# Attention followed by a mixture of experts: temporaries of the token choice in PSUM, the logit add between two scans, and a new written order at a step's and the attention's end

## The chip, the cores and the metric

The kernel runs on one core of one Trainium2 chip. The metric is the device time of one execution in microseconds. A core has five engines with an instruction stream each, which work side by side and wait for one another through semaphores: TensorE (PE, with its weight loads shown apart as PEld), VectorE (DVE), ScalarE (ACT), GpSimd (POOL) and SyncE (SP, here only DMA issues).

## The reference

Two layers follow each other. The first is a gated linear attention with a decay for each channel; the second sends each of 3072 tokens to one of 8 experts, at most 384 to each, in the order of falling logits.

```python
# q, k, v, alpha: (4 batches, 8 heads, 768 positions, 48 channels), float32
for t in range(S):
    state = alpha[:, :, t, :, None] * state + einsum('bhd,bhe->bhde', k[:, :, t], v[:, :, t])
    y[:, :, t] = einsum('bhd,bhde->bhe', q[:, :, t], state)
x = y as (3072, 384)
logits = x @ w_gate                     # (3072, 8)
for idx in argsort(-logits.flatten()):  # greedy: best pair of token and expert first
    tok, e = idx // 8, idx % 8
    if the token has an expert or the expert has 384 tokens: continue
    assigned[tok] = e
for e in range(8):                      # w1: 384 x 1024, w2: 1024 x 384
    out[assigned == e] = relu(x[assigned == e] @ w1[e]) @ w2[e]
```

## The kernel before

**Attention.** The positions are cut into chunks of 128, the heads taken in pairs. A *step* `s` is one pair of heads over four chunks; there are NS = 24 of them, in NG = 6 groups of HP = 4 steps (a group is one set of 512 tokens, its four steps the four pairs). The loop runs over `i`, and in its body stands work of several steps, so that engines overlap:

- PE: the key transposes of step i (`keys`, L237), logits of step i-2 (`logits`, L313), scores of step i (L245), outputs of step i-1 (L294 from the carried state, L300 from the masked scores), and the states of step i (L267).
- DVE: `carry(i-1)` (L283, L285: the running state, chunk by chunk), `add_logits(i-2)` (L319, L321), `decay(i+2)` (two scans over the decays, L211 and L214, with a reciprocal L213 between them), and a piece of the token choice.
- ACT: the scaled states `sb` (L278), the evacuations `kn` (L238), `sm` (L253) and `yt` (L308).
- POOL: the causal mask of step i-1 (L257), the scaled keys and queries of step i+1 (L218, L224), and some clearing of tables (L130).
- SP: the loads of step i+4.

**The token choice.** When a group's four steps have their logits, PE turns them (`turn_logits`, L324), and DVE does the first round of the search ahead of time for these 512 tokens (`first_choice`): the best logit of each token and a one-hot of its expert, the logit's bits as a sortable key, the key cut into five digits, and a table `cmp` that compares the first digit with 128 thresholds. It is a generator with three pieces, one for each loop step: L348 to L351, then L353 to L143 (`digits` is a helper), then L358 and L360. In the step after that, `first_counts` lets PE count with `cmp` as weights (L372) and DVE add the counts up (L377). The last group's choice comes behind the loop.

**PSUM.** One tile `bank` (named `st` in the rows) holds the states' products, the logits, the turned logits and the counts. Another tile, `aux`, has 1024 words a row; 904 of them are filled at the start (zeros and ones, which the scans read, and the reciprocals).

**What sets the order.** Inside `tc.manual_schedule` PE, DVE, ACT and POOL run in the order in which the code is written. Behind the loop, the end of the attention is outside that block: a scheduler orders it. There, `fill(n)` emits `y_trans`, which turns the outputs of a step to token-major form (L332 on PE, L335 on ACT) and every fourth time writes a group to DRAM (L338 on ACT's queue). The numbers `Y_BEFORE_...` say how many of them stand before which part; the rest are spread over the first search (L541 to L623), where four tables are searched one after another. Then eight experts follow, each with gathered rows, weights split into two parts, and two layers of matmuls (L799, L819).

Of the kernel before, what the change touches and what calls it, by code (L numbers as in the profile page):

```python
# [18 lines left out]
WARM_IN_ROUTE = (6, 4, 2, 2)  # L19
Y_BEFORE_CHOICE = 1  # L20
Y_BEFORE_LOGITS = 2
Y_BEFORE_COUNTS = 5
# [6 lines left out]
def gla_moe_kernel(ctx, tc, q, k, v, alpha, w_gate, w1, w2, out):  # L29
# [107 lines left out]

    def digits(key, out_, pool, n):
        di = pool.tile([128, nb, n], I32, name=f"di{n}")
        nc.vector.tensor_tensor(di, key[:, None, :].to_broadcast([128, nb, n]), shifts[:, :, :n],  # L140
                                op=OP.logical_shift_right)
        nc.vector.tensor_tensor(di, di, masks[:, :, :n], op=OP.bitwise_and)
        nc.vector.scalar_tensor_tensor(out_, di, 1.0, scale[:, :, :n], op0=OP.add, op1=OP.mult)  # L143
# [33 lines left out]
    nc.vector.memset(wg, 0.0)  # L177

# [24 lines left out]
    def decay(s):  # L203
# [3 lines left out]
        scans(a, sc, ga, 0, 4)  # L207

    def scans(a, sc, ga, u, n):
# [130 lines left out]
    def first_choice(g):  # L340
        sl = slice(4 * g, 4 * g + 4)
        lw = L[:, sl]
        m = work.tile([128, 4], F32, name="m0")
        val = work.tile([128, 4, E], BF, name="val0")
        sg = work.tile([128, 4], I32, name="sg0")
        key = work.tile([128, 4], I32, name="key0")
        cmp = CM[g] = work.tile([128, T, 4], BF, name="cmp0")
        nc.vector.tensor_copy(lw, lgp[:, :, :E])  # L348
        nc.vector.tensor_reduce(m, lw, axis=mybir.AxisListType.X, op=OP.max)
        nc.vector.tensor_tensor(val, lw, m[:, :, None].to_broadcast([128, 4, E]), op=OP.is_equal)  # L350
        nc.vector.tensor_scalar(sg, m.bitcast(I32), 31, -2 ** 31, op0=OP.arith_shift_right, op1=OP.bitwise_or)  # L351
        yield
        nc.vector.tensor_mul(val, val, ramp_b[:, sl])  # L353
        nc.vector.tensor_tensor(key, m.bitcast(I32), sg, op=OP.bitwise_xor)
# [3 lines left out]
        nc.vector.tensor_tensor(o0[:, sl], ramp_b[:, sl], chu0[:, sl, None].to_broadcast([128, 4, E]),  # L358
                                op=OP.is_equal)
        nc.vector.tensor_tensor(cmp, dig0[:, None, 0, sl].to_broadcast([128, T, 4]), iota, op=OP.is_ge)  # L360
        yield

    def first_counts(g):
        if g == NG - 1:
            fill(Y_BEFORE_COUNTS)
# [4 lines left out]
        with tc.issue_after(YM[NS - len(late) - 1].ins) if last else ExitStack():  # L370
            for u in range(4):
                nc.tensor.matmul(fcp[:, 0 if last else u], CM[g][:, :, u], o0[:, 4 * g + u],  # L372
                                 start=u == 0 or not last, stop=u == 3 or not last)
# [49 lines left out]
    with tc.manual_schedule(engines={E_.DVE, E_.PE, E_.Activation, E_.Pool}):  # L423
# [3 lines left out]
        for i in range(NS + 1):  # L427
# [8 lines left out]
            if i < NS:  # L436
# [6 lines left out]
                keep_scores(i)  # L443
            if i >= 2:
# [21 lines left out]
    fill(Y_BEFORE_LOGITS)  # L466
    logits(NS - 1)
    fill(1)
    add_logits(NS - 1)
    fill(Y_BEFORE_CHOICE)  # L470
    turn_logits(NG - 1)
    for _ in first_choice(NG - 1):
        pass
    first_counts(NG - 1)
# [436 lines left out]
```

## Time and profile before

| | |
|---|---|
| time, median of 3 runs | 462.52 us (461.09 to 462.57) |
| the profiled execution | 460.07 us, its span 458.4 us |
| busy share of the span | PE 89%, PEld 77%, DVE 66%, ACT 43%, POOL 60% |
| granted TensorE clock, mean | 0.948 |
| chain that ended last, by engine | PE 62%, DVE 21%, DMA 6%, issue 6%, ACT 2% |
| attention loop from step 5 to its end | 33.21 to 141.34 us |

"Busy" is the time in which an engine has an instruction in work, a wait for a resource included once it has begun. The chain is followed back from the last instruction, at each step to what released it. In the timeline a row has the start in us from the span's start, the duration in us, engine, line and operation, what is written and read, the count of merged instructions, and in brackets how long the engine was idle before and what ended it. In rows of groups the numbers behind the bar are the busy time in us, the mean of one in ns, and the idle time before.

### The profile page before, as it was taken

To read this page: it belongs to the slowest core of one execution; us is meant where nothing else is said; L and a number is where in the kernel's file an instruction comes from. 1 tells how busy PE (TensorE), PEld (TensorE's weight loads), DVE (VectorE), ACT (ScalarE), POOL (GpSimd) and SP (SyncE) were. 2 spreads that over 40 slices of the span, in tenths; PEclk is the share of its full clock that TensorE was granted. 3 is DMA by queue.
4 is the path that set the end of the run, shared out by engine and by line. 5 is a ranking of instruction groups with operands and counts; after the bars stand their busy time and mean duration, and the time that the engine had idled before them with its cause. 6 is when DMAs were issued, how large, how long until landed. Compare 5 with 4: busy or idle time off the path is not lost.

```text
span 458.4 us, 10845 instructions
## 1 busy us (share of the span) xinstructions
PE 407.5 (89%) x4142; PEld 353.2 (77%) x4142; DVE 304.1 (66%) x837; ACT 196.1 (43%) x447; POOL 275.7 (60%) x300
## 2 busy tenths in 40 slices
PE   7998696968799847997799999999999999899993
PEld 3786575756577734997788889989889889799993
DVE  8789899898963585576558767767768767421210
ACT  2385455545466523416224424524524524444511
POOL 4578776656651006466474964784784786798702
PEclk8599999999999975999899899999999999999998
DMA  8999654653000674136108208108208108920101
GB/s 297 310 264 257 177 164 145 172 165 107 1 4 34 244 259 152 57 101 227 53 1 305 75 1 295 67 19 291 74 19 303 60 19 301 332 73 0 53 2 52
DMA packets 34468, 63.40 MB, mean 138 GB/s; under 512 B 3328, under 2 KB 14592, under 8 KB 34416
## 3 DMA queue, kind: packets, MB, share of 16 engines
q1 hardware_dynamic: 28176, 48.54, 33.4%
q0 software_dynamic: 3072, 9.44, 6.4%
q10 hardware_dynamic: 3168, 4.72, 2.9%
q8 instruction: 33, 0.54, 0.5%
q14 instruction: 19, 0.16, 0.1%
HBM read 53.25 MB, written 9.44 MB: 137 GB/s over the span
## 4 chain that ended last, share of the span: by engine, by line
PE 62%; DVE 21%; DMA 6%; issue 6%; ACT 2%; POOL 1%; POOLq 0%; SPq 0%; DVEq 0%; ACTq 0%
PE h L799 20%; PE y L819 19%; PE rt L590 6%; DVE ga L214 4%; DVE sc L211 4%; DMA raw_a<-in_alpha_dram 4%; PE y L300 3%; DMA xr<-x_dram,idx 3%; PE y L294 3%; PE xt L332 2%; DVE cmp L541 2%; PE xt L783 2%; PE s L245 1%; PE xt L724 1%; PE xt L237 1%
## 5 line engine op out<-in xcount | busy, mean ns | idle before, releaser
L759 POOL TENSOR_TENSOR wlo<-w2r,whi 128x384 fp32r<-128x384 f32 x64 | 64.9, 1015 | 29.9 <-DVE cmp L541 28.4
L803 ACT ACTIVATE hh<-h 128x384 fp32r<-128x384 f32 x64 | 31.4, 491 | 103.0 <-PE h L799 94.1
L759 POOL TENSOR_TENSOR wlo<-w1r,whi 128x384 fp32r<-128x384 f32 x64 | 64.8, 1012 | 8.0 <-ACT whi L753 5.7
L731 POOL DMA_INDIRECT xr<-x_dram,idx x24 | 32.2, 1341 | 62.0 <-DVE scr L648 30.1
L819 PE MATMUL y<-wlo,hh 128*128 128x384 f32 x192 | 66.4, 346 | 0.0
L819 PE MATMUL y<-whi,hh 128*128 128x384 f32 x192 | 66.4, 346 | 0.0
L819 PE MATMUL y<-whi,hl 128*128 128x384 f32 x192 | 65.0, 339 | 0.0
L804 DVE SCALAR_TENSOR_TENSOR hl<-h,hh 128x384 fp32r<-128x384 f32 x64 | 35.5, 554 | 38.8 <-ACT hh L803 34.3
L257 POOL TENSOR_SCALAR_AFFINE_SELECT sm<-sm 128x512 f32<-128x512 f32 x48 | 29.4, 637 | 49.1 <-ACT sm L253 49.1
L753 ACT ACTIVATE whi<-w1r 128x384 fp32r<-128x384 f32 x64 | 32.2, 522 | 53.3 <-PE y L819 37.6
L799 PE MATMUL h<-xh,wlo 128*128 128x384 f32 x192 | 48.8, 354 | 0.0
L799 PE MATMUL h<-xh,whi 128*128 128x384 f32 x192 | 47.0, 352 | 1.9 <-DVE hl L804 0.7
L799 PE MATMUL h<-xl,whi 128*128 128x384 f32 x192 | 48.6, 354 | 0.0
L278 ACT ACTIVATE sb<-st,sc 128x48 f32<-128x48 f32 x80 | 24.5, 331 | 48.1 <-DVE st L285 28.8
L830 POOL DMA_INDIRECT out_dram<-yt,idx x24 | 27.8, 1158 | 26.1 <-ACT yt L823 21.5
L799 PEld LDWEIGHTS h<-xh,whi 128*128 128x128 f32 x192 | 34.3, 194 | 5.6 <-issue 1.8
L541 DVE TENSOR_TENSOR cmp<-nd,iota 128x1536 bf16<-128x1536 bf16 (+4 forms) x32 | 37.4, 1179 | 0.7
L590 PEld LDWEIGHTS <-cmp 128*128 128x128 bf16 x816 | 30.4, 118 | 8.4 <-DVE cmp L541 5.7
L819 PEld LDWEIGHTS y<-wlo,hh 128*128 128x128 f32 x192 | 36.2, 188 | 0.1
L819 PEld LDWEIGHTS y<-whi,hh 128*128 128x128 f32 x192 | 36.1, 188 | 0.1
L819 PEld LDWEIGHTS y<-whi,hl 128*128 128x128 f32 x192 | 36.1, 188 | 0.0
L799 PEld LDWEIGHTS h<-xh,wlo 128*128 128x128 f32 x192 | 35.8, 197 | 0.0
(169 smaller groups left out, 830.8 us busy)
## 6 DMA issues: line engine op xcount, KB each, us to landing
w1r<-in_moe_w_dram SPq DMA_DIRECT2D x16, 768.0 KB, 4.8
w2r<-in_moe_w_dram SPq DMA_DIRECT2D x16, 768.0 KB, 6.4
vt<-in_v_dram SPq DMA_DIRECT2D x24, 256.0 KB, 3.8
x_dram<-xg ACTq DMA_DIRECT2D x6, 768.0 KB, 3.8
raw_a<-in_alpha_dram SPq DMA_DIRECT2D x19, 226.2 KB
raw_k<-in_k_dram SPq DMA_DIRECT2D x19, 224.0 KB
raw_q<-in_q_dram SPq DMA_DIRECT2D x19, 224.0 KB, 3.8
raw_a<-in_alpha_dram SPq DMA_DIRECT2D x5, 258.5 KB, 4.8
```

The lines of the kernel that those rows point to most:

```text
L257: nc.gpsimd.affine_select(SM[s][:, h], SM[s][:, h], pattern=[[0, 4], [1, C]], compare_op=OP.is_ge, fill=0.0, base=0, channel_multiplier=-1)
L278: nc.scalar.activation(SB[s, u][:, :D], St[p], AF.Copy, scale=ac)
L541: x = nc.vector.tensor_tensor(words(dst, nt, js), keyed(d, nt, js), each(iotas[t], nt, js), op=OP.is_ge)
L590: nc.tensor.matmul(cnt, cmp[:, j // U, :, j % U], o[:, j], start=(j == 0), stop=(j == NU - 1))
L731: last_gather[0] = nc.gpsimd.indirect_dma_start(out=XR[i][:, b], out_offset=None, in_=x_dram, in_offset=bass.IndirectOffsetOnAxis(ap=IDX[i ...
L753: nc.scalar.activation(hi[:, 0], a, AF.Copy)
L759: y = nc.gpsimd.tensor_sub(lo[:, h], x, hi[:, h])
L799: nc.tensor.matmul(o, a[:, 0, d], x[:, d], start=(n == 0), stop=(n == 3 * DB - 1))
L803: nc.scalar.activation(hh, o, AF.Relu)
L804: nc.vector.scalar_tensor_tensor(hl, o, 0.0, hh, op0=OP.max, op1=OP.subtract)
L819: F2[i, q] = nc.tensor.matmul(Y[b], a[:, bs], w[:, 1].rearrange("p a b -> p (a b)"), start=(q == 0 and n == 0), stop=(q == FB - 1 and n == 2))
L830: st_ = nc.gpsimd.indirect_dma_start(out=out, out_offset=bass.IndirectOffsetOnAxis(ap=IDX[i][:, b:b + 1], axis=0), in_=yt, in_offset=None)
```

## The change

The temporaries of `first_choice` (the maximum, the one-hot, the key, the digits) and a copy of the small ramp of expert numbers move from SBUF to unused words of `aux` in PSUM; the compare is now an add and a compare in one instruction that reads the digit from there. `add_logits` moves between the first scan and the reciprocal. In a loop step, the scaled keys and queries and the outputs are written ahead of the turn, the choice and the counts. What stood behind the loop is now inside the manual block, with other numbers of `fill`, and the count of the last group has no ordering edge any more.

```diff
+Y_BEFORE_OUTPUTS = 2
+Y_BEFORE_LOGITS = 1
 Y_BEFORE_CHOICE = 1
-Y_BEFORE_LOGITS = 2
-Y_BEFORE_COUNTS = 5
+Y_BEFORE_COUNTS = 4
...
+        nc.vector.tensor_copy(ramp_p, ramp)
+        yield
...
-    def digits(key, out_, pool, n):
...
+    spare = [W4 + 3 * 129]
+
+    def own(n, dt=F32):
+        x = aux[:, spare[0]:spare[0] + n]
+        spare[0] += n
+        return x if dt is F32 else x.bitcast(dt)
+
+    ramp_p, best, key0 = own(E), own(4), own(4, I32)
+    val0 = own(4 * E).rearrange("p (u e) -> p u e", e=E)
+    dig_p = own(nb * 4, I32).rearrange("p (t u) -> p t u", u=4)
...
     def scans(a, sc, ga, u, n, last=-1):
...
+        if last >= 0:
+            add_logits(last)
         nc.vector.reciprocal(aux[:, lo:hi:129], sc[:, lo + 1:hi + 1:129])
...
     def first_choice(g):
...
-        nc.vector.tensor_reduce(m, lw, axis=mybir.AxisListType.X, op=OP.max)
-        nc.vector.tensor_tensor(val, lw, m[:, :, None].to_broadcast([128, 4, E]), op=OP.is_equal)
-        nc.vector.tensor_scalar(sg, m.bitcast(I32), 31, -2 ** 31, op0=OP.arith_shift_right, op1=OP.bitwise_or)
+        nc.vector.tensor_reduce(best, lw, axis=mybir.AxisListType.X, op=OP.max)
+        nc.vector.tensor_tensor(val0, lw, best[:, :, None].to_broadcast([128, 4, E]), op=OP.is_equal)
+        sg = work.tile([128, 4], I32, name="sg0")
+        nc.vector.tensor_scalar(sg, best.bitcast(I32), 31, -2 ** 31, op0=OP.arith_shift_right, op1=OP.bitwise_or)
         yield
-        nc.vector.tensor_mul(val, val, ramp_b[:, sl])
-        nc.vector.tensor_tensor(key, m.bitcast(I32), sg, op=OP.bitwise_xor)
-        nc.vector.tensor_reduce(chu0[:, sl], val, axis=mybir.AxisListType.X, op=OP.max)
-        digits(key, dig0[:, :, sl], work, 4)
+        nc.vector.tensor_mul(val0, val0, ramp_b[:, sl])
+        nc.vector.tensor_tensor(key0, best.bitcast(I32), sg, op=OP.bitwise_xor)
+        nc.vector.tensor_reduce(chu0[:, sl], val0, axis=mybir.AxisListType.X, op=OP.max)
+        nc.vector.tensor_tensor(dig_p, key0[:, None, :].to_broadcast([128, nb, 4]), shifts[:, :, :4],
+                                op=OP.logical_shift_right)
         yield
-        nc.vector.tensor_tensor(o0[:, sl], ramp_b[:, sl], chu0[:, sl, None].to_broadcast([128, 4, E]),
-                                op=OP.is_equal)
-        nc.vector.tensor_tensor(cmp, dig0[:, None, 0, sl].to_broadcast([128, T, 4]), iota, op=OP.is_ge)
+        nc.vector.tensor_tensor(dig_p, dig_p, masks[:, :, :4], op=OP.bitwise_and)
+        nc.vector.scalar_tensor_tensor(dig0[:, :, sl], dig_p, 1.0, scale[:, :, :4], op0=OP.add, op1=OP.mult)
+        nc.vector.tensor_tensor(o0[:, sl], ramp_p[:, None, :].to_broadcast([128, 4, E]),
+                                chu0[:, sl, None].to_broadcast([128, 4, E]), op=OP.is_equal)
+        nc.vector.scalar_tensor_tensor(cmp, dig_p[:, None, 0].to_broadcast([128, T, 4]), 1.0, iota,
+                                       op0=OP.add, op1=OP.is_ge)
         yield
...
-        if g == NG - 1:
-            fill(Y_BEFORE_COUNTS)
...
-        with tc.issue_after(YM[NS - len(late) - 1].ins) if last else ExitStack():
...
             if i >= 2:
-                add_logits(i - 2)
                 if (i - 2) % HP == HP - 1:
                     turn_logits((i - 2) // HP)
-            if i + 2 < NS:
-                decay(i + 2)
-            if i >= 2:
-                if (i - 2) % HP == HP - 1:
                     choosing = first_choice((i - 2) // HP)
                 next(choosing, None)
                 if i > HP + 2 and (i - 2) % HP == 2:
                     first_counts((i - 2) // HP - 1)
-            if 1 <= i < NS - 1:
-                scale_k(i + 1)
-                scale_q(i + 1)
-            if i >= 1:
-                run(outputs(i - 1))
-                emit(i - 1)
```

Ahead of that piece now stand `decay(i + 2, i - 2)` (or `add_logits(i - 2)` where no decay is left), `scale_k` and `scale_q`, at `i == NS` a `fill(Y_BEFORE_OUTPUTS)`, and `outputs(i - 1)` with `emit(i - 1)`; behind it, as before, `states(i)`. The end is, one indent deeper than before:

```python
        fill(Y_BEFORE_LOGITS)
        logits(NS - 1)
        fill(Y_BEFORE_CHOICE)
        add_logits(NS - 1)
        turn_logits(NG - 1)
        for _ in first_choice(NG - 1):
            pass
        fill(Y_BEFORE_COUNTS)
        first_counts(NG - 1)
```

The line numbers of the changed file are 4 to 8 higher. The first place is DVE in step 5, where a group's first choice piece runs, before:

```order
L321 TENSOR_TENSOR lt_180<-lt_180,st 128x128
L211 SCALAR_TENSOR_TENSOR sc<-raw_a_123,aux 128x516
L213 RECIPROCAL aux<-sc 128x4
L214 SCALAR_TENSOR_TENSOR ga<-raw_a_123,aux 128x516
L348 COPY L<-st 128x32
L349 TENSOR_REDUCE m_641<-L 128x4
L350 TENSOR_TENSOR val_642<-L,m_641 128x32
L351 TENSOR_SCALAR sg_643<-m_641 128x4
```

and after (L217, L221, L222 are the scans and the reciprocal, L329 the add, L352 to L356 the piece; `aux` is the PSUM tile):

```order
L217 SCALAR_TENSOR_TENSOR sc<-raw_a_123,aux 128x516
L329 TENSOR_TENSOR lt_180<-lt_180,st 128x128
L221 RECIPROCAL aux<-sc 128x4
L222 SCALAR_TENSOR_TENSOR ga<-raw_a_123,aux 128x516
L352 COPY L<-st 128x32
L353 TENSOR_REDUCE aux<-L 128x4
L354 TENSOR_TENSOR aux<-L,aux 128x32
L356 TENSOR_SCALAR sg_666<-aux 128x4
```

The add has moved behind the first scan, and the piece's results are in `aux`. The second place is PE in the same step, before:

```order
L313 MATMUL st<-yt,wg 32x128 x4
L245 MATMUL s<-qh,kh 128x128 x8
L324 MATMUL st<-ident,lt_180 128x128
L294 MATMUL y<-qh,sb_164 64x128 x2
L294 MATMUL y<-qh,sb_165 64x128 x2
L294 MATMUL y<-qh,sb_167 64x128 x2
L300 MATMUL y<-sm_160,vt 48x128 x4
L300 MATMUL y<-sm_160,vt 64x128 x2
L300 MATMUL y<-sm_160,vt 48x128 x2
L267 MATMUL st<-vt,kn 48x48 x6
```

and after (L302 and L308 are the outputs, L332 the turn, L275 the states):

```order
L253 MATMUL s<-qh,kh 128x128 x8
L302 MATMUL y<-qh,sb_164 64x128 x2
L302 MATMUL y<-qh,sb_165 64x128 x2
L302 MATMUL y<-qh,sb_167 64x128 x2
L308 MATMUL y<-sm_160,vt 48x128 x4
L308 MATMUL y<-sm_160,vt 64x128 x2
L308 MATMUL y<-sm_160,vt 48x128 x2
L332 MATMUL st<-ident,lt_180 128x128
L275 MATMUL st<-vt,kn 48x48 x6
```

The turn has moved from ahead of the outputs to between outputs and states. The third place is PE in step 8, where a group is counted, before:

```order
L267 MATMUL st<-vt,kn 48x48 x6
L237 MATMUL xt<-ident,kh 128x128 x4
L313 MATMUL st<-yt,wg 32x128 x4
L245 MATMUL s<-qh,kh 128x128 x8
L372 LDWEIGHTS cmp_645
L372 MATMUL st<-o_102,cmp_645 128x8
```

and after (L378 is the count):

```order
L253 MATMUL s<-qh,kh 128x128 x8
L302 MATMUL y<-qh,sb_168 64x128 x2
L302 MATMUL y<-qh,sb_169 64x128 x2
L302 MATMUL y<-qh,sb_171 64x128 x2
L308 MATMUL y<-sm_161,vt 48x128 x4
L308 MATMUL y<-sm_161,vt 64x128 x2
L308 MATMUL y<-sm_161,vt 48x128 x2
L378 LDWEIGHTS cmp_662
L378 MATMUL st<-o_102,cmp_662 128x8
```

The counts, which followed the scores, now follow the outputs; each is four weight loads with a matmul.

More of the change, by code (lines that the diff above doesn't have):

```diff
@@ L206, in decay, with scans @@
         ga = GA[s] = work.tile([128, W4], F32, name="ga", bufs=3)
-        scans(a, sc, ga, 0, 4)
-    def scans(a, sc, ga, u, n):
+        scans(a, sc, ga, 0, 4, last)
+    def scans(a, sc, ga, u, n, last=-1):
         lo, hi, top = 129 * u, 129 * (u + n), W4 + 3 * 129
@@ L369, in first_counts @@
             nc.vector.tensor_scalar(need, need, -1.0, float(CAP), op0=OP.mult, op1=OP.add)
-        with tc.issue_after(YM[NS - len(late) - 1].ins) if last else ExitStack():
-            for u in range(4):
-                nc.tensor.matmul(fcp[:, 0 if last else u], CM[g][:, :, u], o0[:, 4 * g + u],
-                                 start=u == 0 or not last, stop=u == 3 or not last)
+        for u in range(4):
+            nc.tensor.matmul(fcp[:, 0 if last else u], CM[g][:, :, u], o0[:, 4 * g + u],
+                             start=u == 0 or not last, stop=u == 3 or not last)
         if last:
@@ L443, in gla_moe_kernel @@
                 keep_scores(i)
+            if i + 2 < NS:
+                decay(i + 2, i - 2)
+            elif i >= 2:
+                add_logits(i - 2)
+            if 1 <= i < NS - 1:
+                scale_k(i + 1)
+                scale_q(i + 1)
+            if i == NS:
+                fill(Y_BEFORE_OUTPUTS)
+            if i >= 1:
+                run(outputs(i - 1))
+                emit(i - 1)
             if i >= 2:
[L445 removed]
                 if (i - 2) % HP == HP - 1:
                     turn_logits((i - 2) // HP)
[L448 to L451 removed]
                     choosing = first_choice((i - 2) // HP)
@@ L465, in gla_moe_kernel @@
                 next(init, None)
[L466 to L474, printed above, removed]
+        fill(Y_BEFORE_LOGITS)
+        logits(NS - 1)
+        fill(Y_BEFORE_CHOICE)
+        add_logits(NS - 1)
+        turn_logits(NG - 1)
+        for _ in first_choice(NG - 1):
+            pass
+        fill(Y_BEFORE_COUNTS)
+        first_counts(NG - 1)
     head = [NS - len(late)]
```

11 lines of the change are left out of this document (1 added, 10 removed).

## Prediction

> **What bounds the kernel now.** I read the page first, for the engines and the chain that ended last.
>
> ```profile
> PE 407.5 (89%) x4142; PEld 353.2 (77%) x4142; DVE 304.1 (66%) x837; ACT 196.1 (43%) x447; POOL 275.7 (60%) x300
> ...
> PE 62%; DVE 21%; DMA 6%; issue 6%; ACT 2%; POOL 1%; POOLq 0%; SPq 0%; DVEq 0%; ACTq 0%
> ```
>
> TensorE (PE) is busy 89% of the span and carries 62% of the chain, VectorE (DVE) 21%. That is a mean over stages that differ. The change touches only the attention stage and its end, so I cut that stage at the PE row that starts a step (the key transposes, L237), in groups of four steps: steps 5 to 8, 9 to 12, 13 to 16, 17 to 20, then 21 to 23. Each row gives length, busy times of PE, PEld, DVE, ACT and POOL, granted clock, DMA share and GB/s.
>
> ```profile
> 33.21:56.17 22.96, 17.85 (x281) 13.89 (x278) 21.45 (x42) 12.69 (x32) 18.14 (x21) 1.00 0.86 217
> 56.17:80.49 24.32, 19.20 (x301) 14.81 (x298) 21.65 (x41) 12.57 (x31) 16.65 (x20) 1.00 0.51 158
> 80.49:104.39 23.90, 18.16 (x292) 14.27 (x290) 21.20 (x45) 12.22 (x29) 14.26 (x17) 1.00 0.57 162
> 104.39:126.90 22.51, 18.71 (x281) 14.99 (x278) 19.75 (x41) 10.89 (x27) 14.32 (x18) 0.94 0.18 55
> 126.90:141.34 14.44, 13.89 (x220) 11.22 (x218) 8.67 (x27) 9.37 (x25) 6.64 (x9) 0.98 0.01 3
> 124.00:127.00 3.00, 3.00 (x37) 2.50 (x34) 1.91 (x4) 1.24 (x3) 2.64 (x4) 0.51 0.00 0
> ```
>
> In the first three groups DVE is busy 89 to 93% and PE 76 to 79%; only in the last, which has no scans left, is PE the fuller one. So DVE sets the pace here. Without a choice on DVE one step takes PE 4.22 us:
>
> ```profile
> 24.86 0.66 PE L237 MATMUL xt<-ident,kh 128*128 128x128 f32 x4
> ...
> 29.08 0.66 PE L237 MATMUL xt<-ident,kh 128*128 128x128 f32 x4
> ```
>
> A group of four at that pace would be 16.9 us, and it takes 22.5 to 24.3. What fills DVE is the token choice. By line, in the window of steps 5 to 23 (busy us, mean ns):
>
> ```profile
> L351 DVE TENSOR_SCALAR sg<-m 128x4 int32<-128x4 int32 x5 | 7.7, 1549 | 0.0
> L360 DVE TENSOR_TENSOR cmp<-dig,iota 128x512 bf16<-128x512 bf16 x5 | 6.2, 1240 | 0.0
> L140 DVE TENSOR_TENSOR di<-key,shifts 128x20 int32<-128x20 int32 x5 | 4.2, 846 | 0.0
> L358 DVE TENSOR_TENSOR o<-ramp_b,chu 128x32 bf16<-128x32 bf16 x5 | 4.1, 826 | 0.0
> L353 DVE TENSOR_TENSOR val<-val,ramp_b 128x32 bf16<-128x32 bf16 x5 | 3.9, 773 | 0.0
> L350 DVE TENSOR_TENSOR val<-L,m 128x32 bf16<-128x32 f32 x5 | 2.7, 532 | 0.2
> ```
>
> These six sum to 28.8 us. The view of each line over the whole run gives least, median and greatest duration:
>
> ```profile
> L350 DVE TENSOR_TENSOR val<-L,m x6: 192/508/674, 38.2 to 148.3; 128x32 bf16<-128x32 f32 x6
> ...
> L351 DVE TENSOR_SCALAR sg<-m x6: 161/1194/2087, 38.7 to 148.4; 128x4 int32<-128x4 int32 x6
> ...
> L353 DVE TENSOR_TENSOR val<-val,ramp_b x6: 166/828/1071, 43.9 to 148.5; 128x32 bf16<-128x32 bf16 x6
> ...
> L140 DVE TENSOR_TENSOR di<-key,shifts x6: 168/1014/1018, 45.0 to 148.8; 128x20 int32<-128x20 int32 x6
> ...
> L358 DVE TENSOR_TENSOR o<-ramp_b,chu x6: 185/894/1094, 49.8 to 148.9; 128x32 bf16<-128x32 bf16 x6
> ...
> L360 DVE TENSOR_TENSOR cmp<-dig,iota x6: 418/1444/1449, 50.7 to 149.5; 128x512 bf16<-128x512 bf16 x6
> ...
> L354 DVE TENSOR_TENSOR key<-m,sg x6: 148/150/156, 44.8 to 148.6; 128x4 int32<-128x4 int32 x6
> ```
>
> The least times belong to the last group, where GpSimd (POOL) has nothing to do. L351 works on 4 elements a row and takes 161 ns there, but up to 2087 among POOL's work. The first five at their least and L360 at 0.418 us would cost 5 x (0.161 + 0.418 + 0.168 + 0.185 + 0.166 + 0.192) = 6.5 us, so 22.3 us of the 28.8 are time in which DVE stands still while POOL runs.
>
> Then the timeline of a group's last step (step 12, with the counts, L372) and of its first (step 9, with the first choice piece):
>
> ```profile
> 73.01 0.66 PE L237 MATMUL xt<-ident,kh 128*128 128x128 f32 x4
> ...
> 76.07 0.85 DVE L285 SCALAR_TENSOR_TENSOR st<-st,sc,st 128x48 f32<-128x48 f32 x3
> ...
> 77.17 0.27 PE L372 MATMUL st<-o,cmp 128*128 128x8 bf16 x4 [2.06 <-DVE lt L321]
> ...
> 79.73 0.16 DVE L377 TENSOR_TENSOR cnt<-cnt,st 128x32 f32<-128x32 f32 x1
> ...
> 79.99 0.56 PE L267 MATMUL st<-vt,kn 128*48 128x48 f32 x16 [0.52 <-issue]
> ...
> 80.49 0.65 PE L237 MATMUL xt<-ident,kh 128*128 128x128 f32 x4
> ```
>
> ```profile
> 56.17 0.66 PE L237 MATMUL xt<-ident,kh 128*128 128x128 f32 x4
> ...
> 57.25 0.87 DVE L285 SCALAR_TENSOR_TENSOR st<-st,sc,st 128x48 f32<-128x48 f32 x3 [1.59 <-PE st L313]
> ...
> 60.92 0.17 DVE L348 COPY L<-st 128x32 f32<-128x32 f32 x1
> ...
> 61.12 0.19 DVE L349 TENSOR_REDUCE m<-L 128x4 f32<-128x32 f32 x1
> ...
> 61.19 0.47 PE L267 MATMUL st<-vt,kn 128*48 128x48 f32 x12 [0.46 <-issue]
> ...
> 61.34 0.67 DVE L350 TENSOR_TENSOR val<-L,m 128x32 bf16<-128x32 f32 x1
> ...
> 61.60 0.65 PE L237 MATMUL xt<-ident,kh 128*128 128x128 f32 x4
> ```
>
> Step 12 takes 7.48 us. Its carry (L285) begins 3.06 us after the step, because DVE is still at the compare of the step before; PE holds the outputs behind the counts for 2.06 us; and the states (L267) start 0.1 us after DVE's L377 ended. Step 9 shows the same tie: L267 follows the end of L348 by 0.1 us. Both DVE reads are of the PSUM tile that the states write, and they stand ahead of the states in program order. The carry of step 9 starts 1.08 us after the step's start: it waits for the logits (L313), writers of the same tile. These ties are not removed by the change.
>
> **The change part by part.**
>
> *Operands in PSUM.* After it no choice instruction has two SBUF inputs: `best`, `val0`, `key0`, `dig_p` and `ramp_p` lie in `aux`. I take the least times for the first five. The compare becomes an add-and-compare with one PSUM operand. Nearest row:
>
> ```profile
> L804 DVE SCALAR_TENSOR_TENSOR hl<-h,hh 128x384 fp32r<-128x384 f32 x64 | 35.5, 554 | 38.8 <-ACT hh L803 34.3
> ```
>
> This instruction of the same kind, with one PSUM input, takes 554 ns for 384 elements a row; at about one element per 1.04 ns (the extra 128 add 133 ns) 512 take 0.69 us, against 0.418 for the undisturbed old form and 1.24 on average. All temporaries now share one tile, so nearly each of the twelve instructions waits for the one before it. L348, L349 and L350 do so already and start 0.20 and 0.22 us apart. So the three pieces cost DVE 4 x 0.215 = 0.86, 0.86 and 0.22 + 0.22 + 0.13 + 0.62 = 1.2 us. Bounds of what DVE is given back per group: all of 22.3 / 5 = 4.5 us less 0.27 for the compare and, as an estimate, 0.05 to 0.1 for each of nine instructions that now wait (0.22 apart, against 0.16 to 0.19 of their own), 3.3 to 3.8 us; or nothing, if the words in PSUM don't keep it from standing still. I take the first, with the three pieces as above, since L354 and the last group show these instructions short when nothing stands in the way.
>
> On the Trainium skill, "SBUF — State Buffer", Who interferes with whom: a DVE instruction with two SBUF inputs, or in a two-port mode, contends with a GpSimd instruction that reads SBUF, and the loser waits the whole instruction; one with a single SBUF input doesn't. L354 has two SBUF inputs and is never stretched (148 to 156 ns), which the page doesn't say by itself; it follows another that has just waited. By the page all 22.3 us go; by L354 alone one can't tell which operand was to blame, so part could stay (a rival below).
>
> *Logits between the scans.* The add moves behind the first scan, into the gap in which the reciprocal waits for it. DVE's chain of carry, add and scans is 60.92 - 57.25 = 3.67 us with three carries, and about 0.3 more with four (0.87 for three). I take 0.1 us off, between 0 and the 0.2 of a dependent start. Who waits for the add: the turn (L324) and the counts, which now come behind the outputs anyway.
>
> *Outputs ahead of turn, choice and counts.* PE no longer holds the outputs for the counts. But turn and counts (0.27 us) now stand between outputs and states, with a DVE answer behind them. They cost nothing while DVE is later than PE there, and it is: DVE reaches L348 3.57 us after the carry.
>
> Now the steps after the change, each from PE's step start.
> - First (turn): carry at 1.08, L348 at 1.08 + 3.57 = 4.65, states 0.27 later, next step 0.41 after that: 5.33 (step 9 now: 5.43).
> - Second and third: PE's own 4.25 to 4.35. DVE needs 2 x 3.57 + 0.86 + 1.2 = 9.2 us in them, PE 8.6, so DVE is 0.6 late at the fourth.
> - Fourth (counts): carry at 1.08 + 0.6 = 1.7, L377 at 5.3, states 0.26 later, next step 0.45 after: 6.0 (step 12 now: 7.48).
>
> That is 5.33 + 4.25 + 4.35 + 6.0 = 19.9 us. In the group of steps 13 to 16 each step has four carries: 0.35 more in the first, and DVE needs 9.8 us against 8.7 in the middle, so the fourth's L377 comes at 6.0 and the step takes 6.75; 5.7 + 4.25 + 4.45 + 6.75 = 21.15. The last three steps lose only the stretch of two pieces: I take 14.05 against 14.44. Sum: 3 x 19.9 + 21.15 + 14.05 = 94.9, against 22.96 + 24.32 + 23.90 + 22.51 + 14.44 = 108.1: **13.2 us less**.
>
> POOL doesn't take over: by the rows above it is busy 14.3 to 18.1 us in a group (the most where it also clears tables), and it waits for ACT's scores, here over the whole run:
>
> ```profile
> POOL sm L257 <- ACT sm L253: 49.1, 24, 5.6
> ```
>
> The loads run several steps ahead of the scans (no DMA wait stands in the window's list), and they are moved past nothing.
>
> *The end, and the clock.* The last group's choice has no POOL beside it, so it only loses:
>
> ```profile
> 147.83 0.19 DVE L348 COPY L<-st 128x32 f32<-128x32 f32 x1 [0.42 <-PE st L324]
> ...
> 149.95 0.29 PE L372 MATMUL st<-o,cmp 128*128 128x8 bf16 x4
> ```
>
> From L348 to the counts it takes 2.12 us; with nine steps of 0.22 and the longer compare about 2.9. Two more instructions (L368, L369) now come behind the compare, at most 0.4, beside PE's counts. Against that the last outputs stand ahead of fewer transposes. Bounds: -0.4 to +1.2; I take +0.3. The row 124 to 127 shows the clock at 0.51 for 3 us, in the count step of its group: 1.5 us lost. The groups before, with the same wait (2.06), stayed at 1.00. My 19.9 for steps 17 to 20 has no such dip, as no PE wait over 1.3 us is left; if one comes all the same, add 1.5. On the Trainium skill, "TensorE: Matmul & The Clock Gate", Part 1: the clock halves after an idle window of about 3.4 us, which free-runs; by it no dip should come after the change, and the sum stays, while the groups without a dip show that such a wait needs the window's position too.
>
> **Sum.** -13.2 + 0.3 = -12.9 us. The profiled execution took 460.07 us (458.4 span), so 447.2 for its like; it lies under all three timed runs, whose median is 462.52: 449.6 there. What follows the attention only moves earlier: same instructions, same order but for transposes beside the search.
>
> **The rivals.**
> - *DVE's time goes, but dependent PSUM instructions are slower than 0.22 us, or one of the five still stands still* (sg still writes SBUF; a piece of 1 us in the third step falls wholly on the fourth). Five choices with 0.5 to 1.5 us more each give back 2.5 to 7.5: 452 to 457. For it: L351, with one SBUF input, is the worst now. Against it: L354 is short, and sg reads PSUM after the change.
> - *The ties don't bind*: states don't wait for L348 and L377 when PE is ready. Then 19 steps at 4.22 plus nine small PE pieces are about 84 us, 24 less: 438 to 443. Rows D and E speak against it.
> - *Nothing freed*: DVE still stands still for POOL, the longer spacing costs 5 x 0.9 = 4.5, and moving the outputs saves about 1 to 1.6 in each of four count steps: 460 to 464.
> - *Slower*: as before, and the turn or counts (0.27, the turn taken alike) with DVE's answer (0.27) now lie bare between outputs and states in nine places: 9 x 0.57 = 5.1 us more, with 4.5 for spacing and nothing saved, 472 at worst, 466 likely. It decides only if less than about 9 of the 22.3 us go.
>
> **How the numbers follow.** 0.3% (1.4 us) is about what this kernel's measurement can tell from no change. Chances: forecast (446 to 452) 0.74, first rival 0.14, ties don't bind 0.05, nothing freed 0.04, slower 0.03. Predicted 449.6. The range 445 to 456 holds the forecast with 1 us of run scatter on the near side, and most of the first rival: about 0.85. Faster 0.95, same 0.02, slower 0.03.
>
> **What would show it.** In the new profile: sg, val, di and o near 0.16 to 0.22 us among POOL's work, the compare near 0.69; groups of 19.9, 19.9, 21.2, 19.9 and 14.0 us; states still 0.1 us behind L348 and L377's successors; no PE wait ahead of the outputs for the counts; clock 1.00 in steps 17 to 20. It is wrong if one of the five stays near 1 us, or if the fourth step stays above 6.8.

## The result, and the profile after

| | before | after |
|---|---|---|
| time, median of 4 runs each, same chip | 462.54 us | 446.62 us (445.79 to 447.99) |
| the profiled execution, its span | 460.07, 458.4 us | 446.41, 444.7 us |
| ratio, 95% interval | | 0.9665 (0.963 to 0.970) |

The kernel is 15.9 us faster; 449.6 us were forecast, in a range of 445 to 456. Medians here and in the table of the experiments are of fast runs: one run each of order_only (462.37 us), states_first_nine (1953 us) and the kernel before (606.67 us, second chip of the experiments) was slow and is left out. The lines of the code stand 4 to 8 further down after the change: key transposes L245, states L275, carry L291 and L293, scans L217 and L222, logit add L329, turn L332, choice L352 to L368, counts L378 and L383, transposes of y L340, the first search's matmuls L597 and L604.

The page of the kernel after, busy times and the chain's engines:

```profile
PE 406.5 (91%) x4142; PEld 352.2 (79%) x4142; DVE 284.5 (64%) x838; ACT 195.7 (44%) x447; POOL 273.8 (62%) x300
...
PE 64%; DVE 11%; issue 8%; DMA 5%; POOL 5%; ACT 4%; POOLq 0%; ACTq 0%; SPq 0%; DVEq 0%
```

DVE's share of the chain falls from 21% to 11%, its busy time from 304.1 to 284.5 us. The groups of steps 5 to 8, 9 to 12, 13 to 16, 17 to 20 and 21 to 23 (length; busy PE, PEld, DVE, ACT, POOL; granted clock; DMA share; GB/s):

```profile
33.48:52.35 18.87, 17.39 (x281) 13.87 (x278) 16.29 (x42) 12.92 (x33) 17.00 (x20) 1.00 0.99 249
52.35:72.04 19.69, 18.44 (x301) 14.84 (x298) 16.08 (x41) 12.57 (x31) 17.52 (x21) 1.00 0.65 194
72.04:92.69 20.65, 18.28 (x292) 14.15 (x289) 16.91 (x45) 12.21 (x29) 14.23 (x17) 1.00 0.64 190
92.69:111.55 18.86, 17.39 (x280) 13.88 (x277) 15.48 (x41) 11.32 (x28) 13.94 (x17) 1.00 0.20 62
111.55:125.51 13.96, 13.48 (x220) 10.98 (x217) 7.68 (x27) 8.92 (x23) 7.12 (x10) 1.00 0.01 3
```

The groups are 92.0 us together, against 108.1: **16.1 us less**. DVE is busy 15.5 to 16.9 us in a full group, against 19.8 to 21.7, and PE is now the fuller engine. The clock stays at 1.00, in steps 17 to 20 too, where it had been 0.94. The choice's instructions, over the whole run (least, median, greatest ns):

```profile
L356 DVE TENSOR_SCALAR sg<-aux x6: 161/161/161, 38.6 to 132.1; 128x4 int32<-128x4 int32 x6
...
L358 DVE TENSOR_TENSOR aux<-aux,ramp_b x6: 190/200/200, 43.1 to 132.3; 128x32 f32<-128x32 f32 x6
...
L361 DVE TENSOR_TENSOR aux<-aux,shifts x6: 186/186/186, 43.8 to 132.9; 128x20 int32<-128x20 int32 x6
...
L366 DVE TENSOR_TENSOR o<-aux,chu x6: 180/180/181, 47.7 to 133.5; 128x32 bf16<-128x32 f32 x6
...
L368 DVE SCALAR_TENSOR_TENSOR cmp<-aux,iota x6: 681/681/681, 47.7 to 133.6; 128x512 bf16<-128x512 int32 x6
```

What had medians of 508 to 1444 ns now takes the same time beside POOL's work as without it. The count step of the first group (step 8):

```profile
46.81 0.66 PE L245 MATMUL xt<-ident,kh 128*128 128x128 f32 x4
...
47.33 0.19 DVE L364 TENSOR_TENSOR aux<-aux,masks 128x20 int32<-128x20 int32 x1
...
47.75 0.68 DVE L368 SCALAR_TENSOR_TENSOR cmp<-aux,iota 128x512 bf16<-128x512 int32 x1
...
48.35 0.25 DVE L293 SCALAR_TENSOR_TENSOR st<-st,sc,st 128x48 f32<-128x48 f32 x1
...
48.94 1.22 DVE L217 TENSOR_TENSOR_SCAN sc<-raw_a,aux 128x516 f32<-128x516 f32 x1
...
50.07 0.26 DVE L329 TENSOR_TENSOR lt<-lt,st 128x128 f32<-128x128 f32 x1
50.25 0.18 DVE L221 RECIPROCAL aux<-sc 128x4 f32<-128x4 f32 x1
...
50.69 0.29 PE L378 MATMUL st<-o,cmp 128*128 128x8 bf16 x4
...
51.68 0.16 DVE L383 TENSOR_TENSOR cnt<-cnt,st 128x32 f32<-128x32 f32 x1
...
51.94 0.47 PE L275 MATMUL st<-vt,kn 128*48 128x48 f32 x12 [0.96 <-ACT sb L286]
...
52.35 0.44 PE L245 MATMUL xt<-ident,kh 128*128 128x128 f32 x2
```

The carry starts 1.54 us after the step (3.06 in this step and in step 12 of before), and from there DVE runs without a gap to the count add; the logit add stands between the scan and the reciprocal. The counts (L378) come behind the outputs, and the states still start 0.1 us after the count add ends. So they do after the turn, in step 5:

```profile
37.91 0.17 DVE L352 COPY L<-st 128x32 f32<-128x32 f32 x1
...
38.17 0.47 PE L275 MATMUL st<-vt,kn 128*48 128x48 f32 x12 [0.51 <-ACT yt L316]
```

Not all of the 16.1 us arrive. By stages of the two profiled executions, in us: start of step 5 +0.3; steps 5 to 23 -16.1; from there to the first row of L604 +0.2; **from its first row to its fifth, the first search, 14.0 against 12.8, +1.2**; to the first gather 0.0; the rest +0.7 (287.4 us; the same kernel took 284.6 there on another chip, so no cause is sought). That sums to -13.7, the difference of the spans; the medians differ by 2.2 us more, since the profiled execution of before was a quick one (460.07 against 462.54).

Where the search loses, on PE and on ACT:

```profile
138.72 1.54 PE L340 MATMUL xt<-ident,yt 128*128 128x128 f32 x9
140.59 0.66 PE L340 MATMUL xt<-ident,yt 128*128 128x128 f32 x4 [0.33 <-ACT xg L343]
141.09 0.93 PE L597 MATMUL rt<-o,cmp 128*128 128x8 bf16 x24
```

```profile
139.58 0.37 ACTq L346 DMA_DIRECT2D x_dram<-xg  x1
140.05 0.87 ACT L343 ACTIVATE xg<-xt 128x384 f32<-128x384 f32 x2 [0.50 <-ACT xg L343]
```

PE does nine transposes, waits for ACT's copy `xg`, does four more, and only then come the next counts (L597). ACT's copy is late because its queue issues the transfer of `x_dram` (L346) right ahead of it. Before, one more transposed step stood ahead of the last counts, and there the issue fell beside the search's counts:

```profile
154.15 1.98 PE L332 MATMUL xt<-ident,yt 128*128 128x128 f32 x13
155.97 0.92 PE L590 MATMUL rt<-o,cmp 128*128 128x8 bf16 x24
...
156.69 0.37 ACTq L338 DMA_DIRECT2D x_dram<-xg  x1
```

The thirteen transposes, with the wait among them, take 2.53 us after and 1.98 before.

### The profile page after: what moved, and what is told of

Same layout as the page of the kernel before. It is cut to its first block, busy times and chain, and to the rows that moved or that the text cites. A ratio compares the mean times of both kernels' runs of the same rounds, so it can differ in the third digit from the quotient of the medians.

```text
span 444.7 us, 10850 instructions
## 1 busy us (share of the span) xinstructions
PE 406.5 (91%) x4142; PEld 352.2 (79%) x4142; DVE 284.5 (64%) x838; ACT 195.7 (44%) x447; POOL 273.8 (62%) x300
## 4 chain that ended last, share of the span: by engine, by line
PE 64%; DVE 11%; issue 8%; DMA 5%; POOL 5%; ACT 4%; POOLq 0%; ACTq 0%; SPq 0%; DVEq 0%
PE h L806 17%; PE y L826 15%; PE rt L597 6%; PE y L308 5%; PE s L253 5%; PE y L302 5%; POOL wlo L766 3%; DMA xr<-x_dram,idx 3%; PE xt L245 3%; DVE cmp L548 2%; PE st L275 2%; PE st L321 2%; PE xt L790 2%; DMA w2r<-in_moe_w_dram 2%; PE xt L731 1%
## 5 line engine op out<-in xcount | busy, mean ns | idle before, releaser
L738 POOL DMA_INDIRECT xr<-x_dram,idx x24 | 30.7, 1277 | 63.4 <-DVE scr L655 31.5
L597 PEld LDWEIGHTS <-cmp 128*128 128x128 bf16 x816 | 30.4, 118 | 8.6 <-DVE cmp L548 5.7
L806 PEld LDWEIGHTS h<-xl,whi 128*128 128x128 f32 x192 | 35.5, 197 | 0.3
```

The source lines that it names most:

```text
L597: nc.tensor.matmul(cnt, cmp[:, j // U, :, j % U], o[:, j], start=(j == 0), stop=(j == NU - 1))
L738: last_gather[0] = nc.gpsimd.indirect_dma_start(out=XR[i][:, b], out_offset=None, in_=x_dram, in_offset=bass.IndirectOffsetOnAxis(ap=IDX[i ...
L806: nc.tensor.matmul(o, a[:, 0, d], x[:, d], start=(n == 0), stop=(n == 3 * DB - 1))
```

## The experiments

They ran in three sets on three chips, each beside runs of the kernel before. "Loop" is from the start of step 5 to the start of the last states, "search" from the first to the fifth row of L604 or its like, both from the profile.

| kernel | time us | before there | ratio, 95% interval | loop | search |
|---|---|---|---|---|---|
| before (first chip) | 462.54 | | | 107.8 | 12.8 |
| after (first chip) | 446.62 | 462.54 | 0.9665 (0.963 to 0.970) | 91.7 | 14.0 |
| psum_only | 443.97 | 459.60 | 0.9665 (0.9616 to 0.9713) | 94.2 | 13.4 |
| order_only | 455.61 | 459.60 | 0.9922 (0.9888 to 0.9956) | 105.0 | 13.8 |
| add_ahead | 445.61 | 459.60 | 0.9703 (0.9666 to 0.9740) | 94.1 | 14.7 |
| nine_y | 442.05 | 459.60 | 0.9624 (0.9584 to 0.9663) | 91.9 | 12.8 |
| states_first | 439.82 | 462.18 | 0.9493 (0.9456 to 0.9530) | 83.4 | 14.6 |
| states_first_nine | 438.43 | 462.18 | 0.9494 (0.9445 to 0.9543) | 83.3 | 12.8 |
| no_pool_products | 453.01, one | 462.18 | | 90.4 | 15.4 |
| after_again | 442.85 | 459.33 | 0.9635 (0.9604 to 0.9665) | 91.6 | 14.0 |
| x_on_sp | 442.28 | 459.33 | 0.9611 (0.9575 to 0.9647) | 91.9 | 13.1 |
| states_first_x_on_sp | 434.80 | 459.33 | 0.9472 (0.9431 to 0.9514) | 83.3 | 13.1 |
| val_back | 443.08, one | 459.33 | | 92.7 | 14.4 |

The same kernel differs by up to 3.8 us between chips, so times are compared within a set. The loop tells more than the time: in the four kernels whose loop is the same (after, after_again, nine_y, x_on_sp) it is 91.6 to 91.9 us.

The search is less steady, and not only by its order. At a granted clock of 1.00 throughout it took 12.8 to 14.0 us. In add_ahead, val_back and states_first one of its steps ran at a clock of 0.58 to 0.67 and took 0.5 to 0.6 us longer than in the kernel after; in no_pool_products two did, at 0.60. Thirteen transposes in states_first, 1.98 us in the row of before above:

```profile
131.01 3.11 PE L340 MATMUL xt<-ident,yt 128*128 128x128 f32 x13
```

The step ahead of them is alike in states_first and after (PE busy 2.82 of 3.82 us and 2.80 of 3.81), so why the clock fell in one of them only stays open. A search of more than 14.0 us is therefore no measure of an order.

**psum_only.** The kernel before, with `own`, `ramp_p` and the new operands in `first_choice`; its three pieces cut where they were, its order and end as they were.

```diff
+    ramp_p, best, key0 = own(E), own(4), own(4, I32)
+    val0 = own(4 * E).rearrange("p (u e) -> p u e", e=E)
+    dig_p = own(nb * 4, I32).rearrange("p (t u) -> p t u", u=4)
...
-        nc.vector.tensor_tensor(cmp, dig0[:, None, 0, sl].to_broadcast([128, T, 4]), iota, op=OP.is_ge)
+        nc.vector.scalar_tensor_tensor(cmp, dig_p[:, None, 0].to_broadcast([128, T, 4]), 1.0, iota,
+                                       op0=OP.add, op1=OP.is_ge)
```

> The kernel before with only its choice operands in PSUM; the order of a step and the end as before. Theory (the gain is DVE no longer standing still for POOL, and the order matters little): with DVE only 1.5 us late in a count step the counts find the add done before PE reaches them, so the old order costs nothing; it lacks 0.1 us a step from the add between the scans (about 1.5 us) and has the old end and search (1.1 + 0.2 us shorter): 446 to 448.5, choice rows 0.16 to 0.2 us. Rival (the order carries a part of its own, 1 to 1.6 us in each of four count steps, as the prediction had it): 450 to 453.

The ratio is that of the whole change, the loop 13.6 us shorter than before. So the operands carry most of the gain by themselves. The rival (450 to 453 us, a ratio of 0.973 to 0.979) is out.

**order_only.** The kernel after, with the old temporaries in SBUF (`m`, `val`, `key`, `di`, and the compare from `dig0`).

> The kernel after with its choice temporaries back in SBUF (the old forms of the instructions, in the new order and the new end). Theory: DVE stands still as before (sg over 1 us, compare near 1.4), its row of carry, scans and choice stays without a gap up to the count add, so the step ends when it did before; 1.5 us less for the add between the scans, 1.3 more for end and search: 461 to 463. Rival 1 (outputs ahead of the counts save 1 to 1.6 us in four steps): 456 to 458. Rival 2 (turn and counts lie bare ahead of the states): 466 to 468.

4.0 us by the medians (2.0 to 5.1 by the interval): more than the theory's number, less than rival 1's. The loop says which: its count steps take 7.26, 7.39, 7.59 and 7.27 us, those of before 7.20, 7.48, 7.52 and 7.55, so nothing of 1 to 1.6 us is saved there. What is saved, 2.8 us in the loop, is 0.14 to 0.2 us in each turn step of a full group, 0.4 in the last, and up to 0.6 in some of the steps between. There the digits' last two instructions have moved to the third piece; that this is the cause was not shown by itself. So the theory's mechanism stands (DVE stands still and its row has no gap up to the count add), but its size was too small, and of the two rows that it named only one stays long: sg has a median of 1193 ns, the compare one of 425. Its step 8:

```profile
50.11 0.26 DVE L293 SCALAR_TENSOR_TENSOR st<-st,sc,st 128x48 f32<-128x48 f32 x1
...
50.85 0.66 PE L302 MATMUL y<-qh,sb 64*64 64x128 f32 x8 [1.52 <-ACT sb L286]
...
53.44 0.16 DVE L386 TENSOR_TENSOR cnt<-cnt,st 128x32 f32<-128x32 f32 x1
...
53.71 0.47 PE L275 MATMUL st<-vt,kn 128*48 128x48 f32 x12 [0.96 <-ACT sb L286]
```

PE no longer waits for the counts, but it waits 1.5 us for `sb`, which hangs on the same late carry; and DVE, from the carry (L293) to the count add (L386), runs as ever, with the states 0.1 us behind.

**add_ahead.**

```diff
+            if i >= 2:
+                add_logits(i - 2)
             if i + 2 < NS:
-                decay(i + 2, i - 2)
-            elif i >= 2:
-                add_logits(i - 2)
+                decay(i + 2, -1)
```

> The kernel after with the logits added ahead of the two scans again. Theory: the add costs DVE about 0.1 us a step more there; the turn and count steps end by DVE, and the middle ones hand their lateness to the count step: 4 groups x 0.4 = 1.6 us more, 448.0 to 448.5, turn steps 5.2, count steps 5.8 to 5.9. Rival (the gap behind the first scan was free for nobody, or the lateness is absorbed): 446.6, no difference. Rival 2 (0.2 us a step, a whole dependent start): 449.8.

The turn steps take 5.24 to 5.76 us (5.10 to 5.61 after), the count steps 5.97, 6.17, 6.30 and 5.96 (5.54, 5.74, 6.00 and 5.53), the two between the same but for one (4.95 for 4.82); the loop is 2.4 us longer. Its step 8, from 46.50:

```profile
48.33 0.25 DVE L293 SCALAR_TENSOR_TENSOR st<-st,sc,st 128x48 f32<-128x48 f32 x1
...
51.80 0.16 DVE L383 TENSOR_TENSOR cnt<-cnt,st 128x32 f32<-128x32 f32 x1
```

From the carry to the count add it is 3.47 us, against 3.33 after: 0.14 us for the add. In a count step it shows three times, since the two middle steps hand theirs on: 0.43 us. The theory, with 0.14 in the place of 0.1, by the loop; by the times it can't be told (the intervals of add_ahead and after overlap). Between psum_only (94.2) and this kernel (94.1) lie the outputs ahead of turn and counts, and the two digit instructions in the third piece: together they are worth nothing in the loop.

**no_pool_products.** The kernel before; `scale_k` and `scale_q` give the raw keys and queries, so POOL's two products of a step, and the scaling, are left out.

```diff
     def scale_k(s):
+        KH[s] = raw["k", s]
+        return
```

> The kernel before with POOL's two products of a step left out (keys and queries are used unscaled from step 2 on; DVE's instructions are those of before). Theory (the choice instructions are stretched by POOL's two-input products beside them): sg, the compare and the shift fall from medians of 1.19, 1.44 and 1.01 us to near their least, 0.16, 0.42 and 0.17, unless POOL's masking, which stays, stretches them too; total below 455. Rival (they are stretched by DMA writes, or by something of DVE's own): the medians stay over 0.8 us.

```profile
L354 DVE TENSOR_TENSOR val<-L,m x6: 191/192/194, 43.7 to 136.8; 128x32 bf16<-128x32 f32 x6
...
L355 DVE TENSOR_SCALAR sg<-m x6: 160/164/337, 43.9 to 136.9; 128x4 int32<-128x4 int32 x6
...
L364 DVE TENSOR_TENSOR cmp<-dig,iota x6: 416/418/424, 52.8 to 138.0; 128x512 bf16<-128x512 bf16 x6
```

All are near their least but two of L355 (0.21 and 0.34 us). The loop is 90.4 us, as short as that of the whole change, with the old operands and in the old order: POOL's products are what stretched DVE. POOL's masking stays, but here no choice instruction of steps 5 to 12 runs beside it, so what it would do is not shown. The time does not show the gain in full, because a step ahead of step 5 takes 9.6 us (PE waits 3.0 us in it for the load of `raw_q` and then runs at a clock of 0.57; that the load is late because PE reads the raw buffers later and so frees them later was only argued) and the search 15.4, two of its steps at a clock of 0.60. The longer of the two stretched rows:

```profile
61.97 0.95 POOL L130 MEMSET cmp<- 128x1024 bf16 x1
...
62.50 0.19 DVE L354 TENSOR_TENSOR val<-L,m 128x32 bf16<-128x32 f32 x1
62.61 0.34 DVE L355 TENSOR_SCALAR sg<-m 128x4 int32<-128x4 int32 x1
```

Beside POOL's MEMSET, L354 with two SBUF inputs takes 0.19 us, and L355, a TENSOR_SCALAR with one SBUF input, 0.34: it ends 0.03 us after the MEMSET does (62.92). By the Trainium skill, "SBUF — State Buffer", Who interferes with whom, two SBUF inputs contend with a GpSimd instruction that reads SBUF, not with one that only writes, and a `tensor_scalar` can run in a two-port mode, which contends with GpSimd. The row of L354 agrees; that of L355 does if L355 runs in such a mode, which no run here shows by itself.

**val_back.**

```diff
-    val0 = own(4 * E).rearrange("p (u e) -> p u e", e=E)
+    val0 = rc.tile([128, 4 * E], F32, name="val0").rearrange("p (u e) -> p u e", e=E)
```

> The kernel after with one operand, val0, back in SBUF (float, one tile). Theory (an instruction stands still when it reads two SBUF operands beside a product of POOL's, and a result written to SBUF does no harm): the product val0 x ramp_b (L358) is stretched, median 0.5 to 1.1 us, while the compare that writes val0 (L353, one SBUF input) and the maximum that reads it (L360, one input) stay at 0.19 to 0.2 us; at most 2.5 us more in the attention. Rival (any touch of SBUF, the write too, is enough): L353 is stretched as well. Rival 2 (one operand alone is not worth anything): L358 at 0.2.

The compare that writes `val0` stands in L354; the expectation named L353, the maximum, which took 194 to 195 ns.

```profile
L354 DVE TENSOR_TENSOR val<-L,aux x6: 187/188/190, 37.4 to 131.9; 128x32 f32<-128x32 f32 x6
...
L358 DVE TENSOR_TENSOR val<-val,ramp_b x6: 167/562/1043, 42.1 to 132.1; 128x32 f32<-128x32 f32 x6
...
L360 DVE TENSOR_REDUCE chu<-val x6: 186/186/186, 43.1 to 132.3; 128x4 f32<-128x32 f32 x6
```

The theory: the instruction with two SBUF inputs (L358) is stretched, up to 1043 ns; the one that writes to SBUF (L354) and the one that reads one operand (L360) aren't. The loop is 1.0 us longer, within the 2.5 expected and beyond the 0.2 by which equal loops differ. This one operand is a small part of the 13.6.

**states_first.**

```diff
             if i >= 1:
                 run(outputs(i - 1))
                 emit(i - 1)
+            if i < NS:
+                run(states(i))
             if i >= 2:
                 if (i - 2) % HP == HP - 1:
                     turn_logits((i - 2) // HP)
...
-            if i < NS:
-                run(states(i))
```

> The kernel after with the states' matmuls written ahead of turn, choice and counts (behind the outputs). Theory (turn and count steps are long because the states wait for DVE's reads of the turn and the counts, which stand ahead of them in the order and lie in the same PSUM tile, though they don't need them): turn and count steps fall from 5.1 to 5.3 and 5.5 to 6.0 us to about 4.5, groups from 18.9 to 20.7 to about 17.5 to 18, the last by 0.8: 7 to 8 us less, 438 to 441. Rival 1 (DVE's own work sets these steps; the tie only names what was last): at most 2 us less, 445 to 447. Rival 2 (the tie moves to the logits and the carry of the next step, which write and read the same tile, and take the whole of it): 446 to 448.

```profile
34.02:50.98 16.96, 16.96 (x281) 14.02 (x278) 15.81 (x41) 12.41 (x32) 15.94 (x19) 1.00 1.07 255
50.98:68.98 18.00, 17.85 (x301) 14.81 (x300) 16.34 (x42) 12.88 (x33) 17.58 (x21) 1.00 0.99 245
68.98:87.26 18.28, 17.73 (x294) 14.14 (x292) 16.51 (x46) 11.92 (x29) 13.96 (x17) 1.00 0.69 207
87.26:104.38 17.12, 16.78 (x281) 13.84 (x280) 15.63 (x42) 11.32 (x29) 14.03 (x17) 1.00 0.27 79
104.38:117.79 13.41, 13.16 (x221) 10.99 (x219) 8.51 (x29) 9.42 (x25) 8.35 (x11) 1.00 0.01 3
```

```profile
37.77 0.44 PE L275 MATMUL st<-vt,kn 128*48 128x48 f32 x12
...
38.14 0.33 PE L332 MATMUL st<-ident,lt 128*128 128x128 f32 x1
...
38.51 0.19 DVE L352 COPY L<-st 128x32 f32<-128x32 f32 x1
```

Step 5 takes 4.28 us in the place of 5.10, step 8 4.27 in the place of 5.54; PE is busy 100% of the first group. The other turn and count steps take 4.3 to 4.8 us. The loop loses 8.3 us more. DVE's answer (L352) now runs beside the next step's key transposes. The theory holds; neither rival does.

**nine_y, x_on_sp and after_again.** `Y_BEFORE_COUNTS = 5`; and `nc.sync.dma_start` in the place of `nc.scalar.dma_start` for `x_dram`.

> The kernel after with five instead of four transposes of y ahead of the first counts of the last group, so nine stand ahead of the search as before. Theory (the search is 1.1 us longer because the transposes in it now stand so that ACT's issue of the x_dram transfer falls inside each search step): the search is 12.8 us again, total 445.4 to 445.9. Rival (something else in the search, or the transpose that is taken out of the search is paid in full ahead of the counts): 446.6 to 447.2.

> The kernel after with the x_dram transfers issued on SP's queue instead of ACT's. Theory (ACT's issue between two of its copies is what makes the eight-transpose search longer): PE's waits for ACT's xg inside a search step go, first to last L604 of the search 12.8 to 13.2 us instead of 13.97, 1 us less in all. Rival (what matters is how many transposes lie between two counts, not the issue): the search stays at 13.9 and the time with it. Rival 2 (SP's weight loads now wait behind the transfer): the time after the gather grows, total equal or more.

> The kernel after, unchanged, beside the three others of this set on one chip, as their measure: 0.9665 of the kernel before, 444 to 447 us.

after_again came out at 0.9635 and 442.85 us, 1.2 us under its range; 0.9665 is the edge of its interval. The search is 12.8 and 13.1 us, against 14.0: with one more transposed step ahead, or with the issue on another queue, most of the loss goes, as the theory says. But x_on_sp is no clean test of the queue, since PE's order changed with it: between the turn and the last counts it runs 24 transposes, where the kernel after runs 16, and in the search three transposes stand between the two halves of a count.

```profile
130.39 3.72 PE L340 MATMUL xt<-ident,yt 128*128 128x128 f32 x24
```

So the row of the kernel after, where PE waits 0.33 us for a copy with the issue right ahead of it, shows the issue's part; that it is the whole 1.2 us is argued. The stage from the last states to the first L604 is 0.1 and 0.4 us longer, so 1.1 and 0.4 are left. The number of transposes alone does not fix it: psum_only, with nine of them in the order of before, took 13.4. In the times it can't be told: x_on_sp 442.28 against 442.85, intervals overlapping. Of SP's weight loads no loss is seen: from the first gather to the end it takes 285.2 us, against 284.6 in after_again and 285.3 in nine_y, where the queue is as it was.

**states_first_nine, states_first_x_on_sp.** Both edits together, in two ways.

> The same with nine transposes of y ahead of the search. Theory: both gains add, 1.0 us under the kernel with the states first alone: 437 to 440. Rival (the end comes out of step with the transposes in another way): the same time as that kernel.

> States ahead of turn, choice and counts, eight transposes ahead of the search, and the x_dram transfers on SP's queue. Theory: 7.5 us under the kernel after from the states and 1 us more from the search: 0.947 to 0.949 of before. Rival (the issue is not the cause): 0.951 to 0.952, as with the states first alone.

Both searches come back (12.8 and 13.1, against 14.6, of which the low clock is 0.6). states_first_nine is not faster than states_first by its ratio, so that both gains add is not shown in the time. states_first_x_on_sp, whose order on PE changed as that of x_on_sp did, is the fastest of all: 434.80 us, 8.05 less than the kernel after on the same chip; its ratio came out where the theory put it, but the step from states_first lies within the intervals.

## Why the prediction was right, and where its sizes were off

- *Operands in PSUM*: right. DVE stood still for POOL's products (no_pool_products), reading two SBUF operands is enough (val_back), and no instruction of the choice is stretched after. So the first rival (one of the five still stands still), "nothing freed" and "slower" are out.
- *The spacing of 0.22 us and the compare of 0.69*: the compare is 0.68. The second piece takes 0.76 and the third 1.02 us until the carry starts (47.33 to 48.35 above), against 0.86 and 1.2: the carry starts before the compare has ended.
- *DVE's chain, 3.57 us for three carries*: this is the first term that was mis-sized. It was read in step 9 (3.67) and used for all groups. Before, it was 3.47 already in the first group:

```profile
52.03 0.25 DVE L285 SCALAR_TENSOR_TENSOR st<-st,sc,st 128x48 f32<-128x48 f32 x1
...
55.50 0.16 DVE L377 TENSOR_TENSOR cnt<-cnt,st 128x32 f32<-128x32 f32 x1
```

  There two of the three carries are multiply-adds and one is a copy; after, it is 3.33. So the lateness of 0.6 at the fourth step was 0.46, the first step 5.10 and not 5.33, the fourth 5.54 and not 6.0. The second and third, put at 4.25 and 4.35, took 4.12 and 4.11: these groups have less PE work (281 matmuls in the row of steps 5 to 8, 301 in that of steps 9 to 12, where the two took 4.33 and 4.34). The chain accounts for 0.7 us of such a group, the two middle steps for 0.4, and the groups of steps 5 to 8 and 17 to 20 came out at 18.9 for 19.9. Steps 9 to 12, where the chain fits (3.52), came out at 19.7 for 19.9; steps 13 to 16 at 20.7 for 21.15. Sum -16.1 for -13.2.
- *The add between the scans*, 0.1 us a step: 0.14, and 2.4 us in the loop, since three steps of a group add up.
- *Outputs ahead of turn and counts cost nothing while DVE is later*: right, and they bring nothing either. In the rival "nothing freed", the 1 to 1.6 us that moving them was to save in each count step are wrong: order_only doesn't show them.
- *The ties stay*: right, at 0.1 us, so the rival "the ties don't bind" is out; states_first shows their price, 8.3 us.
- *The end, +0.3*: +0.2. The step that failed is "what follows the attention only moves earlier: same instructions, same order but for transposes beside the search". Those transposes decide where ACT's issue falls; the search lost 1.2 us, most of which came back in nine_y.
- *The clock*: no dip in steps 17 to 20, as forecast.
- *Slips of the working*: 0.57 a place in the rival "slower" should be 0.27 + 0.27 = 0.54, so 4.9 us and not 5.1; the "Rows D and E" of the second rival are the rows of steps 12 and 9. Neither moves the forecast.

That the forecast of -12.9 lay near the spans' -13.7 is in part luck: the groups gave 2.9 us more than forecast, and the search (1.2), the start (0.3) and the stretch behind the gather (0.7), which the sum held at nothing, took most of that away. The -15.9 of the medians are 2.2 us more, by where the profiled execution of before stands among its runs; the prediction had carried -12.9 over to the median unchanged.

## What to carry to other kernels

When small DVE instructions take several times their length beside GpSimd's products, move one of their two operands to PSUM (of sg, the only one); a result in SBUF did no harm here. After that, ask which instruction stands behind another engine's answer for the sake of a shared tile only: writing the states ahead of the turn and the counts took another 8.3 us off the loop, half of what the whole change had taken (16.1). And where an interleaved stretch has a period, moving one piece out of it shifts everything behind it against the queues, so its length has to be worked out anew.

## What the runs showed that was not expected

- In order_only, `key` (two SBUF inputs, 148 to 156 ns in before) has a median of 654 ns and takes up to 1199, and the compare, whose median was 1444, has one of 425. In step 8 the compare now runs beside POOL's MEMSET (from 49.64 us for 0.95) and no longer beside a product. So which instruction stands still depends on where POOL's product falls, and the least length of one row is no evidence on its operands.
- A TENSOR_SCALAR with one SBUF input is stretched even beside POOL's MEMSET (0.34 us for 0.16, row above).
- The first search took 12.8 to 15.4 us with the same instructions: 12.8 to 14.0 by the order of the transposes, the counts and ACT's issue in it, and more where the granted clock fell to about 0.6 in one or two of its steps.
